# Own-key blocks of a squared-relu attention: half of the second step's weights read back turned from DRAM instead of computed

## The chip, the cores and the metric

The kernel runs on one core of a Trainium2 chip. The time is the device time of one execution in microseconds. Before the change it was 1749.55 us, the median of 3 runs (1749.34 to 1753.78). All profile rows come from one profiled execution. PE is TensorE's matmuls, PEld its weight loads, DVE VectorE, ACT ScalarE, POOL GpSimd, SP SyncE; SPq is SyncE's DMA queue.

## The reference

Eight batches of 2496 rows. Attention takes z both as queries and as keys, so its scores are symmetric, and then each row goes past a gate to one of eight experts:

```python
scores = (1.0 / S) * np.matmul(z, z.transpose(0, 2, 1))   # z: 8 x 2496 x 64
attn = np.maximum(scores, 0.0) ** 2
x = (u * np.matmul(attn, v)).reshape(B * S, D)            # u, v: 8 x 2496 x 256

do_compute = x @ w_skip > 0                               # rows that go to an expert
e_idx = np.argmax(x[do_compute] @ w_gate, axis=1)         # 8 experts, 256 -> 1024 -> 256
y = gate_w * (np.maximum(xc @ w1[e], 0.0) @ w2[e])
out[do_compute] = x[do_compute] + y                       # the other rows: out = x
```

All inputs are fp32. The kernel keeps nearly fp32 accuracy on TensorE by splitting each operand into a high and a low part and adding three products: high by high, high by low, low by high.

## The kernel before

**Attention, the first 1200 us or so.** A batch's queries are cut into 5 chunks (0 to 4), four of 512 and the last of 448. The keys come in 10 groups of 256, called p; so there are 8 x 5 x 10 = 400 steps, each one chunk of queries against one group of keys. The key groups p = 2c and p = 2c+1 are the chunk's own keys: the block in which keys and queries are the same rows of z. ORDER gives the order of the ten steps of a chunk; for chunks 1 to 4 the own group 2c is the first step (k = 0) and 2c+1 the last (k = 9).

A step makes its weights and then uses them:

- `scores`: six matmuls 64x512 (L277) give the scores of 256 keys by 512 queries in PSUM, `ps`. Each product runs on two 64-row halves of TensorE, which hold different keys.
- ScalarE takes the relu into the tile `r` (L325, 128x1024 in fp32) and squares it (L326).
- The high part `ah` is a cast of `r` (L335, on ScalarE or VectorE as `on_act` says); the low part `al` is the difference (L339, VectorE).
- `attend` (L366): twelve matmuls for each half d of the 256 columns of v, with `ah` or `al` streaming into the accumulators `acc`.

Weights are made two steps ahead of their use (`LA = 2`), by `stage`. There are 5 buffers for `r`, 3 each for `ah` and `al`, 2 in PSUM for `ps`.

**Symmetry between chunks.** The weights of keys in block j by queries in block c are the transpose of those of keys in c by queries in j. So the chunk that comes first computes its block, VectorE turns it in 32x32 pieces (`keep`, L294, tile `rt`), four puts of 256 KB write it to a DRAM tile `kept` (L728, by `put_some`, which is called once at the end of a step and issues at most four puts, of entries that are at least one step old, two in chunks 1 to 4), and the chunk that comes later reads it back ready (`recall`, L310, or L312 and L313 for the last chunk of 448), with no scores, relu or square. The recall is issued by `ahead(s + LA + 3)`, five steps before the step that uses it and three before that step's weights are staged. The own blocks are not in this scheme: both own-key steps of a chunk compute all their scores. In batch 0, the first chunk's blocks are not kept.

**What sets the order.** All engines' programs are recorded in the order of the code; each engine runs its own in that order. All transfers of `r`, `rt`, the loads of u and v (L168, L97), the rows stored after a chunk (L416 in four puts of 128 KB with 256-byte pieces, L412) are issued by SyncE, whose queue also keeps that order. A chunk's rows are stored at step 4 of the next chunk.

**The end of a chunk.** At k = 9 the accumulators are copied out (L394, ScalarE, into `xrow`, and L396, VectorE) and turned (L403); the next chunk's first two steps are staged around that.

**The MoE part, to the end.** Rows are gathered by expert through index lists; h (L638) and y (L657) are three matmuls per product, again high and low; relu (L643, ScalarE) and its low part (L644, VectorE).

Of the kernel before, what the change touches and what calls it, by code (L numbers as in the profile page):

```python
# [8 lines left out]
F32 = mybir.dt.float32  # L9
# [3 lines left out]
AF = mybir.ActivationFunctionType  # L13
# [4 lines left out]
P = 128  # L18
QC = 512
# [4 lines left out]
NFIX = 3  # L24
HT = 64
NARM = 4 * (NSTAT - NFIX)
NWARM = 52

# [14 lines left out]
def f32(ap):  # L45
    return ap.bitcast(F32)
# [3 lines left out]
def attn_moe(ctx, tc, zT, uT, v, wg, w1, w2, cst, pad, out):  # L50
# [4 lines left out]
    nc = tc.nc  # L55
    B, _, SZ = zT.shape
    S = uT.shape[3]
    D = 2 * P
# [5 lines left out]
    isc = 1.0 / S  # L64

    chunks = []
# [5 lines left out]
    dram = ctx.enter_context(tc.tile_pool(name="dram", bufs=1, space=bass.MemoryType.DRAM))  # L72
    vp = ctx.enter_context(tc.tile_pool(name="vp", bufs=1))
# [14 lines left out]
    zt, vt = {}, {}  # L88
# [85 lines left out]
    ones = cpool.tile([P, P], BF16, name="ones")  # L174
    nc.gpsimd.memset(ones, 1.0)
    psw = ps_s.tile([P, 2, QC], F32, name="psw", tag="s")
    for _ in range(NWARM):
        nc.tensor.matmul(psw[:32, 0, :70], ones[:, :32], ones[:, :70], start=True, stop=True)

    f0 = load_z(0, 0, nc.vector)  # L180
    f1 = load_v(0, 0, nc.vector)
# [59 lines left out]
        return (j, c) in pairs(b) or (c, j) in pairs(b) or p in EXTRA[c]  # L241

    kept = {x: dram.tile([QC, QC], F32, name="kept%d%d" % x) for x in PAIRS}
    HALF = (slice(0, 64), slice(64, 128))

    zq = {}

# [13 lines left out]
    def queries(ci, k, h, n):  # L261

        if ci in zq:
            return zq[ci][k][h, :n]
        return zt[ci // NQ, ci % NQ][k][h].rearrange("p (b a i) -> p a b i", b=4, a=4)

    def scores(ci, p):

# [11 lines left out]
    def r_tile():  # L280
        return ap.tile([P, 2, QC], F32, name="r", tag="r", bufs=5)
# [3 lines left out]
    def keep(ci, p, r):  # L285
# [12 lines left out]
        if p % 2:  # L298

            dst = kept[c, j].rearrange("(m i) k -> i m k", i=32)  # L300
            for a in range(4):
                puts.append((step[0], dst[:, :, a * P : a * P + P], t[32 * a : 32 * a + 32]))

    def recall(ci, p):

        r = r_tile()
        src = kept[p // 2, ci % NQ].rearrange("(k p) q -> p k q", k=4)
        src = src[:, p % 2 * 2 : p % 2 * 2 + 2, :]
        if chunks[ci][2] == QC:
            nc.sync.dma_start(r, src)  # L310
        else:
            nc.sync.dma_start(r[:, :, :352], src[:, :, :352])  # L312
            nc.sync.dma_start(r[:, :, 352:448], src[:, :, 384:480])  # L313
        return r
# [3 lines left out]
    def weights(ci, p, r=None, at_end=False):  # L318

        b, q0, n = chunks[ci]  # L320
        old, new = r, (ci % NQ, p // 2) in pairs(b)
        if not old:
            ps = scores(ci, p)
            r = r_tile()
            nc.scalar.activation(r[:, :, :n], ps[:, :, :n], AF.Relu, scale=isc)  # L325
            nc.scalar.activation(r[:, :, :n], r[:, :, :n], AF.Square)  # L326
        views, got = [], []

        def high():
            ah = ap.tile([P, 2, QC], F32R, name="ah", tag="ah")  # L330
            al = ap.tile([P, 2, QC], F32R, name="al", tag="al")
            got.extend((ah, al))
            views.append([x[:, :, :n] for x in (r, ah, al)])
            for r_, h_, _ in views:
                (nc.scalar.copy if on_act(ci, p) else nc.vector.tensor_copy)(h_, r_)  # L335

        def low():
            for r_, h_, l_ in views:
                nc.vector.tensor_sub(l_, r_, f32(h_))  # L339
            if new:  # L340
                if at_end:
                    put_off.append(lambda: keep(ci, p, r))
                else:
                    keep(ci, p, r)

        return got, high, low
# [383 lines left out]
    def ahead(s):  # L730
        if s < len(steps):
            ci, p = steps[s]
            if (p // 2, ci % NQ) in pairs(ci // NQ):
                old[s] = recall(ci, p)
                known.add(s)


    def later(s, k, load, *args):
        def start():
# [57 lines left out]
    for s, (ci, p) in enumerate(steps):  # L797
        b, q0, n = chunks[ci]
        k = s % NP
        step[0] = s  # L800
        ahead(s + LA + 3)
        if k == 0:
            accs[ci] = [[ps_acc.tile([P, QC], F32, name="acc", tag="acc") for _ in range(2)] for _ in range(2)]
        acc = accs[ci]
        if k < NP - 1:
            high, low = stage(s + LA)
            if k < NP - 2 or s + LA in known:
                high()
                low()
                high = low = lambda: None  # L810
            while k == NP - 3 and put_off:
                put_off.pop()()
            attend(b, n, p, 0, acc[0], *aa[s], k == 0, False)
            for t in () if k in (0, NP - 2) else (s - 1, s) if k == 1 else (s,):
                attend(b, n, steps[t][1], 1, acc[1], *aa.pop(t), t % NP == 0, False)
            rest = high, low
        else:


            part, mul, rows0, rows1, store = finish(ci)  # L820
            attend(b, n, p, 0, acc[0], *aa[s], False, True)

            high, low = rest
            if s + 1 < len(steps) and not on_act(*steps[s + 1]):
                high()
                low()
                high = low = lambda: None
            part(0, 1, acc[0])
            part(0, 0, acc[0])
            high()  # L830
            low()
            high, low = stage(s + LA)
            attend(b, n, steps[s - 1][1], 1, acc[1], *aa.pop(s - 1), False, False)
            if s + LA in known:

                high()
                low()
                high = low = lambda: None
            attend(b, n, p, 1, acc[1], *aa.pop(s), False, True)
            part(1, 1, acc[1])  # L840
            high()
            part(1, 0, acc[1])
            low()
            mul()
            accs.pop(ci)

            new.append(ci)
            if ci < NC - 1:
                after = [(rows0, 2), (rows1, 3), (store, 4), (store, 8)]
                if ci % 2 == 0:  # L850
                    gates, logits, route, counts, gate, place, put_in = routing(new)
                    after = [(gates, 2), (logits, 2), (rows0, 2), (rows1, 3), (route, 4), (counts, 4),
                             (store, 4), (gate, 5), (place, 6), (store, 8)]
                    for t in range(0, 4 * len(new), 2):
                        f = lambda put_in=put_in, t=t: put_in(t, t + 2)
                        if s + 6 + t < len(steps):
                            after.append((f, 6 + t))
                        else:
                            left.append(f)
                    new = []  # L860
                for f, k in after:
                    todo.setdefault(s + k, []).append(f)
            else:
                gates, logits, route, counts, gate, place, put_in = routing(new, False)
        for f in todo.pop(s, []):
            f()
        put_some()
# [200 lines left out]
```

## Time and profile before

| | |
|---|---|
| profiled execution | 1750.08 us, span 1748.3 us |
| runs | 1749.55 us median (1749.34 to 1753.78) |
| mean granted TensorE clock | 0.998 |
| TensorE busy | 1729.9 us, 99% of the span |
| VectorE, ScalarE, GpSimd busy | 1187.8, 1131.5, 519.8 us |
| scores, relu and square | 248 times each on ScalarE |
| full recalls | 90 of 512 KB, median 6.5 us from issue to landing |
| puts of turned blocks | 304 of 256 KB, median 4.8 us |

In a row of a timeline the first number is the start in us from the span's start, the second the length, then engine, line, operation, tiles (output <- input), shape and how many instructions the row stands for; in brackets the idle time before it and what ended that. For a DMA the row is its issue, not its transfer. A row of a window gives its bounds and length, busy time of PE, PEld, DVE, ACT and POOL with instruction counts, the granted clock, the mean busy share of the DMA engines, and GB/s. A row of the waits gives the total idle time, the number of waits and the longest.

### The profile page before, as it was taken

The page shows a single profiled execution, that of the slowest core. Times are in us where ns is not written, and L with a number is a line of the kernel's source. Part 1 is how long each engine was busy: PE and PEld are TensorE (multiplying, and loading weights), DVE is VectorE, ACT ScalarE, POOL GpSimd, SP SyncE. Part 2 cuts the span into 40 slices and gives each one's busy share as a digit, 9 for nine tenths or more (in the row PEclk, how much of TensorE's full clock was granted, in tenths as well). Part 3 has the DMA queues.
Part 4 walks back from the last instruction along what each step waited for, and adds up shares of the span by engine and source line. Part 5 has one row for each costly group of instructions (what it writes and reads, how often), then busy time and mean ns, then how long its engine had stood idle before and what let it go on. Part 6 is the DMA issues. An engine that isn't in the chain of part 4 may idle for free. (4 is left out here: it accounts for less than half of the span.)

```text
span 1748.3 us, 39163 instructions
## 1 busy us (share of the span) xinstructions
PE 1729.9 (99%) x15476; PEld 1531.0 (88%) x15476; DVE 1187.8 (68%) x1928; ACT 1131.5 (65%) x1409; POOL 519.8 (30%) x516
## 2 busy tenths in 40 slices
PE   9999999999999999999999999999999999999998
PEld 7888788988888898888889888888999999999997
DVE  7877877887887788788778877877753334344332
ACT  8877877887687778768787876887533323333321
POOL 1103202212311221231222032122256456635731
PEclk9999999999999999999999999999999999999999
DMA  5566779577867858885785888586653333323310
GB/s 194 151 180 173 187 209 275 136 221 233 216 167 202 251 162 231 230 234 148 206 250 163 212 240 228 138 223 190 202 128 81 86 88 106 91 59 97 85 42 26
DMA packets 373514, 294.71 MB, mean 169 GB/s; under 512 B 136432, under 2 KB 311409, under 8 KB 372560
## 3 DMA queue, kind: packets, MB, share of 16 engines
q1 hardware_dynamic: 359136, 267.85, 55.4%
q0 software_dynamic: 13632, 22.99, 4.6%
q8 instruction: 137, 2.24, 0.5%
q14 instruction: 177, 1.45, 0.3%
q10 hardware_dynamic: 432, 0.18, 0.0%
HBM read 177.92 MB, written 133.79 MB: 178 GB/s over the span
## 5 line engine op out<-in xcount | busy, mean ns | idle before, releaser
L366 PE MATMUL acc<-ah,vh 64*128 64x512 f32 (+1 forms) x3120 | 641.5, 384 | 2.7 <-DVE ah L335 2.0
L366 PE MATMUL acc<-ah,vl 64*128 64x512 f32 (+1 forms) x3120 | 626.4, 382 | 0.0
L339 DVE TENSOR_TENSOR al<-r,ah 128x1024 fp32r<-128x1024 f32 (+1 forms) x400 | 479.2, 1204 | 169.6 <-ACT ah L335 163.1
L366 PE MATMUL acc<-al,vh 64*128 64x512 f32 (+1 forms) x3120 | 498.2, 384 | 1.9 <-DVE al L339 1.2
L537 POOL DMA_INDIRECT lst<-pair,dest x160 | 200.0, 1250 | 769.1 <-DVE dest L535 685.1
L335 ACT CAST ah<-r 128x1024 fp32r<-128x1024 f32 (+1 forms) x356 | 362.8, 1030 | 80.9 <-PE acc L366 43.4
L366 PEld LDWEIGHTS acc<-ah,vh 64*128 64x128 f32 x3120 | 326.8, 184 | 56.0 <-ACT ah L335 4.3
L366 PEld LDWEIGHTS acc<-ah,vl 64*128 64x128 f32 x3120 | 327.1, 184 | 44.5 <-DVE vl L122 0.3
L366 PEld LDWEIGHTS acc<-al,vh 64*128 64x128 f32 x3120 | 309.5, 184 | 56.3 <-DVE al L339 11.7
L325 ACT ACTIVATE r<-ps 128x1024 f32<-128x1024 f32 (+1 forms) x248 | 252.7, 1019 | 147.2 <-PE ps L277 129.1
L643 ACT ACTIVATE hh<-psh 128x512 fp32r<-128x512 f32 (+2 forms) x172 | 97.0, 571 | 282.6 <-PE psh L638 261.2
L326 ACT ACTIVATE r<-r 128x1024 f32<-128x1024 f32 (+1 forms) x248 | 261.4, 1054 | 7.9
L657 PE MATMUL y<-w2t,hh 128*128 128x256 f32 (+1 forms) x1328 | 235.0, 280 | 0.0
L644 DVE SCALAR_TENSOR_TENSOR hl<-psh,hh 128x512 fp32r<-128x512 f32 (+2 forms) x172 | 110.2, 655 | 146.7 <-ACT hh L643 130.2
L294 DVE STREAM_TRANSPOSE rt<-r 128x512 f32<-128x512 f32 x304 | 197.3, 687 | 9.4 <-DMA kept<-rt 8.5
L657 PEld LDWEIGHTS y<-w2t,hh 128*128 128x128 f32 (+1 forms) x1328 | 200.5, 185 | 1.3
L638 PE MATMUL psh<-xt,w1h 128*128 128x256 f32 (+3 forms) x896 | 184.6, 303 | 2.9 <-DVE hl L644 2.9
L657 PE MATMUL y<-w2t,hl 128*128 128x256 f32 (+1 forms) x664 | 184.2, 277 | 0.0
L638 PEld LDWEIGHTS psh<-xt,w1h 128*128 128x128 f32 x896 | 141.7, 189 | 8.5 <-DVE hl L644 4.4
L638 PE MATMUL psh<-xt,w1l 128*128 128x256 f32 (+3 forms) x448 | 135.0, 301 | 0.0
L689 POOL DMA_INDIRECT out<-o,idt x77 | 76.5, 994 | 164.2 <-DVE o L686 131.9
L657 PEld LDWEIGHTS y<-w2t,hl 128*128 128x128 f32 (+1 forms) x664 | 122.6, 185 | 0.0
(188 smaller groups left out, 1706.7 us busy)
## 6 DMA issues: line engine op xcount, KB each, us to landing
kept<-rt SPq DMA_DIRECT2D x304, 256.0 KB, 4.8
r<-kept SPq DMA_DIRECT2D x90, 512.0 KB, 6.5
r<-kept SPq DMA_DIRECT2D x62, 352.0 KB, 5.6
raw<-in_v SPq DMA_DIRECT2D x80, 256.0 KB, 5.5
ut<-in_uT SPq DMA_DIRECT2D x32, 512.0 KB, 5.8
xr<-xrow SPq DMA_DIRECT2D x128, 128.0 KB, 3.1
out<-xr SPq DMA_DIRECT2D x32, 512.0 KB, 6.8
raw<-in_w SPq DMA_DIRECT2D x64, 256.0 KB, 3.3
```

Source lines behind the costliest of these rows:

```text
L294: nc.vector.transpose(t[:, :, 32 * k : 32 * k + 32].rearrange("p (k a) i -> p a k i", k=4), r[:, x, :].rearrange("p (a k i) -> p a k i", a ...
L325: nc.scalar.activation(r[:, :, :n], ps[:, :, :n], AF.Relu, scale=isc)
L326: nc.scalar.activation(r[:, :, :n], r[:, :, :n], AF.Square)
L335: (nc.scalar.copy if on_act(ci, p) else nc.vector.tensor_copy)(h_, r_)
L339: nc.vector.tensor_sub(l_, r_, f32(h_))
L366: nc.tensor.matmul(acc[t][:, :n], w[h, x, dd], a[h, x, :n], start=(first and t not in halves[:m]), stop=(last and t not in halves[m + 1 :]),)
L537: put = nc.gpsimd.indirect_dma_start(out=lst, out_offset=bass.IndirectOffsetOnAxis(ap=dest[:, t : t + 1], axis=0), in_=pair[:, t, :], in_o ...
L638: nc.tensor.matmul(ps[:, j * W : (j + 1) * W], wt[:, a, o : o + P], x[:, d, :W], start=(m == 0), stop=(m == 5),)
L643: nc.scalar.activation(hh[:, : G * W], ps[:, : G * W], AF.Relu)
L644: nc.vector.scalar_tensor_tensor(hl[:, : G * W], ps[:, : G * W], 0.0, f32(hh[:, : G * W]), op0=ALU.max, op1=ALU.subtract)
L657: nc.tensor.matmul(ys[t], h[:, tt], w2t[f][:, k, :], start=(f == 0 and m == 0 and t % share == 0), stop=(f == NF - 1 and m == 2), skip_gro ...
L689: put = nc.gpsimd.indirect_dma_start(out=out, out_offset=bass.IndirectOffsetOnAxis(ap=ids[:m, t, 0:1], axis=0), in_=ot, in_offset=None, bo ...
```

## The change

The own block is symmetric in itself. With its 512 rows split in two, the first own-key step (keys 0 to 255, p = 2c) holds among others the weights of keys 0 to 255 by queries 256 to 511; turned, they are those of keys 256 to 511 by queries 0 to 255, which is half of the second own-key step (p = 2c+1). For chunks 1, 2 and 3 of every batch (24 places) the change

- turns that half at the end of the first own-key step (`keep_half`, two VectorE transposes of 128 partitions by 256, into a tile `rd` that takes a buffer of the loads' tag "raw") and puts it to a DRAM tile of 256x256 by four puts of 64 KB, through the same list of puts;
- reads it into the lower half of the second own-key step's `r` (`recall_half`, two DMAs of 128 KB whose pieces in SBUF are 256 bytes), issued by `half_ahead(s + LA + 1)`, three steps before the use, right behind the full recall that `ahead` issues in the same step;
- computes scores for the other half of the queries alone (`scores_half`, six matmuls of 256 columns in place of 512), with relu and square of half the size. The cast and everything behind it are as before, on the whole tile.

The warming matmuls at the start go from 52 of 70 columns to 53 of 69.

```diff
+    kept_d = {c: dram.tile([QC // 2, QC // 2], F32, name="kept%d" % c) for c in range(1, S // QC)}
+    def own(ci, p):
+        b, c = ci // NQ, ci % NQ
+        return p % 2 if c in kept_d and p // 2 == c else None
+    def upper(x):
+        return x.rearrange("p x (a j) -> p x a j", a=4)[:, :, :, 64:]
+    def scores_half(ci, p):
+        b, _, _ = chunks[ci]
+        ps = ps_s.tile([P, 2, QC], F32, name="ps", tag="s")
+        zh, zl = zt[b, p // 2]
+        for m, (k, q) in enumerate(((zh, 0), (zh, 1), (zl, 0))):
+            for x, h in enumerate(HALF):
+                o = (2 * p + x) % 4 * P
+                nc.tensor.matmul(
+                    ps[:, x, : QC // 2].rearrange("p (a j) -> p a j", a=4), k[h, o : o + P],
+                    queries(ci, q, h, QC).rearrange("p (a j) -> p a j", a=4)[:, :, 64:],
+                    start=(m == 0), stop=(m == 2),
+                )
+        return ps
+    def keep_half(ci, r):
+        c = ci % NQ
+        t = vp.tile([P, 2, D], F32, name="rd", tag="raw", bufs=4).rearrange("p x (k i) -> p (x k) i", i=64)
+        for x in range(2):
+            nc.vector.transpose(
+                t[:, :, 32 * x : 32 * x + 32].rearrange("p (k a) i -> p a k i", k=2),
+                r[:, x, :].rearrange("p (a k i) -> p a k i", a=4, k=4)[:, :, 2:],
+            )
+        dst = kept_d[c].rearrange("(m i) k -> i m k", i=32)
+        for a in range(4):
+            puts.append((step[0], dst[:, :, 64 * a : 64 * a + 64], t[32 * a : 32 * a + 32]))
+    def recall_half(ci):
+        r = r_tile()
+        for x in range(2):
+            nc.sync.dma_start(
+                r[:, x].rearrange("p (a j) -> p a j", a=4)[:, :, :64],
+                kept_d[ci % NQ][x * P : x * P + P].rearrange("p (a j) -> p a j", a=4),
+            )
+        return r
...
-        if not old:
+        if own(ci, p) == 1:
+            ps = scores_half(ci, p)
+            part = ps[:, :, : QC // 2].rearrange("p x (a j) -> p x a j", a=4)
+            nc.scalar.activation(upper(r), part, AF.Relu, scale=isc)
+            nc.scalar.activation(upper(r), upper(r), AF.Square)
+        elif not old:
...
+            if own(ci, p) == 0:
+                todo.setdefault(step[0] + 1, []).append(lambda: keep_half(ci, r))
...
+    def half_ahead(s):
+        if s < len(steps) and own(*steps[s]) == 1:
+            old[s] = recall_half(steps[s][0])
...
         ahead(s + LA + 3)
+        half_ahead(s + LA + 1)
```

SyncE's queue in chunk 1 of batch 4, before: the rows of the chunk ahead (xr, L416), four puts of a turned block, then a full recall, the load of u and further recalls. (The numbers behind `kept_` count DRAM tiles, and are one higher after the change.)

```order
L416 DMA xr<-xrow 32x16x64 x4
L728 DMA kept_195<-rt 32x16x128 x4
L310 DMA r<-kept_191 128x2x512
L168 DMA ut<-in_uT 128x2x512
L310 DMA r<-kept_191 128x2x512
L412 DMA out<-xr 16x8192
```

The same place after the change:

```order
L472 DMA xr<-xrow 32x16x64 x4
L784 DMA kept_201<-rd 32x8x64 x4
L784 DMA kept_196<-rt 32x16x128 x4
L359 DMA r<-kept_192 128x2x512
L347 DMA r<-kept_201 128x4x64 x2
L168 DMA ut<-in_uT 128x2x512
L359 DMA r<-kept_192 128x2x512
L468 DMA out<-xr 16x8192
```

The four puts of the half (`kept_201<-rd`) stand ahead of the four of the whole block; its two reads stand behind the full recall and ahead of u.

SyncE's queue in chunk 2 of the same batch, before:

```order
L97 DMA raw<-in_v 128x512
L416 DMA xr<-xrow 32x16x64 x4
L728 DMA kept_197<-rt 32x16x128 x4
L310 DMA r<-kept_192 128x2x512
L168 DMA ut<-in_uT 128x2x512
L310 DMA r<-kept_195 128x2x512
L412 DMA out<-xr 16x8192
```

and after:

```order
L784 DMA kept_202<-rd 32x8x64 x4
L97 DMA raw<-in_v 128x512
L472 DMA xr<-xrow 32x16x64 x4
L784 DMA kept_198<-rt 32x16x128 x4
L359 DMA r<-kept_193 128x2x512
L347 DMA r<-kept_202 128x4x64 x2
L168 DMA ut<-in_uT 128x2x512
L359 DMA r<-kept_196 128x2x512
L468 DMA out<-xr 16x8192
```

Here the puts of the half go out ahead of a load of v and of the rows; the two reads again stand right behind the full recall.

More of the change, by code (lines that the diff above doesn't have):

```diff
@@ L26 @@
 NARM = 4 * (NSTAT - NFIX)
-NWARM = 52
+NWARM = 53
 PAIRS = ((0, 1), (0, 2), (0, 3), (0, 4), (1, 2), (1, 3), (1, 4), (2, 3), (2, 4), (3, 4))
@@ L177, in attn_moe @@
     for _ in range(NWARM):
-        nc.tensor.matmul(psw[:32, 0, :70], ones[:, :32], ones[:, :70], start=True, stop=True)
+        nc.tensor.matmul(psw[:32, 0, :69], ones[:, :32], ones[:, :69], start=True, stop=True)
     f0 = load_z(0, 0, nc.vector)
```

## The prediction

> **What bounds the kernel now.** I read the page's busy times first, then the stages by window, and then the timeline of each engine around the own-key steps of the three middle chunks. The page says that TensorE has almost no idle time (first row; the second, from the chain of waits, prices a matmul of 256 columns):
>
> ```profile
> PE 1729.9 (99%) x15476; PEld 1531.0 (88%) x15476; DVE 1187.8 (68%) x1928; ACT 1131.5 (65%) x1409; POOL 519.8 (30%) x516
> 1626.95 5.46 PE y L657 x48
> ```
>
> So every column that TensorE no longer streams is time, and every moment for which it waits is time too. The change does both: it takes columns away and gives TensorE a transfer to wait for. The two must be priced apart.
>
> **The gain per place.** The six score matmuls of an own-key step stand as three rows of two ahead of the next attend row (chunk 2 of batch 4, TensorE's timeline):
>
> ```profile
> 724.40 0.39 PE L277 MATMUL ps<-zqh,zh 64*128 64x512 f32 x2
> ...
> 725.08 0.39 PE L366 MATMUL acc<-ah,vh 64*128 64x512 f32 x2
> ```
>
> From 724.40 to 725.08 are 0.68 us, 0.227 a pair; the two matmuls of a pair use different 64-row halves and run side by side. At 256 columns no pair is in this trace; the nearest row is the chain's 5.46 us for 48 matmuls of 128x256, 0.114 each. If a pair goes down to that, a place saves 3 x (0.227 - 0.114) = 0.34 us. There are 24 places (8 batches, chunks 1 to 3): **8.2 us**. The lower bound is no gain, if the weight loads, which are as many as before, don't fit behind a matmul of half the length. What a load takes is seen where one could not hide, behind a stall:
>
> ```profile
> 1098.37 0.47 PE L366 MATMUL acc<-ah,vh 64*128 64x448 f32 x2 [1.18 <-DVE ah L335]
> 1098.68 0.36 PE L366 MATMUL acc<-ah,vl 64*128 64x448 f32 x2
> ```
>
> The first pair is 0.11 us longer than the second: two loads of 64x128 side by side cost 0.11, just less than 0.114. I take the full 0.34, and keep 0 for the range. The Trainium skill ("TensorE: Matmul & The Clock Gate", Part 3) says that a weight load overlaps with matmuls in flight only when its row group differs. By that rule a pair here would take load and matmul one after the other, 0.11 + 0.23 = 0.34; the trace disagrees, with 0.227. At 256 columns that rule would leave 0.11 + 0.114 = 0.22 a pair and no gain.
>
> **What moves to other engines.** VectorE gets two more transposes of half a tile at the end of the first own-key step; the whole one is 0.69 us, so the two are between 0.7 and 1.4 (half price, or no gain from the smaller size). ScalarE's relu and square go from 1.03 and 1.06 to the size of the 0.57 row: about 0.95 us less a place.
>
> ```profile
> L294 DVE STREAM_TRANSPOSE rt<-r 128x512 f32<-128x512 f32 x304 | 197.3, 687 | 9.4 <-DMA kept<-rt 8.5
> L643 ACT ACTIVATE hh<-psh 128x512 fp32r<-128x512 f32 (+2 forms) x172 | 97.0, 571 | 282.6 <-PE psh L638 261.2
> 681.32 1.23 DVE L339 TENSOR_TENSOR al<-r,ah 128x1024 fp32r<-128x1024 f32 x1 [1.38 <-ACT ah L335]
> ```
>
> VectorE idles 1.38 us in the third row, ahead of the low part at the start of chunk 1, and that cover takes the transposes; uncovered they would delay the next low part by at most 1.4 us. I take 0. The saving on ScalarE counts only if the cast behind it may start, and this cast now waits for the recalled half. That is the term that decides.
>
> **When the half comes back.** SyncE's queue issues in program order, and the new transfers stand there: four puts of 64 KB in 256-byte pieces, and two reads of 128 KB of which each lands in 256-byte pieces, placed right behind the chunk's full recall (L310). Nearest prices:
>
> ```profile
> r<-kept SPq DMA_DIRECT2D x90, 512.0 KB, 6.5
> 714.00:717.00 3.00, 3.00 (x30) 2.49 (x28) 1.39 (x2) 2.97 (x4) 0.54 (x1) 1.00 0.80 166
> 719.00:723.00 4.00, 4.00 (x38) 3.33 (x36) 2.04 (x3) 3.94 (x5) 0.00 (x0) 1.00 0.81 190
> 726.00:728.00 2.00, 2.00 (x20) 1.68 (x18) 0.58 (x1) 1.94 (x3) 1.77 (x4) 1.00 0.98 342
> ```
>
> (The last three are windows; the last two numbers are the DMA engines' busy share and GB/s.) 714 to 717 is the store of rows in 256-byte pieces: 166 GB/s at 0.80, so 208 at full share. 719 to 723 is puts in 512-byte pieces, 235 at full share; 726 to 728 reads in 2-KB pieces, 342 at 0.98. So 256 KB of 256-byte pieces occupy the engines for 1.26 us (0.75 at the read rate, the lower bound). The Trainium skill ("DMA: Bandwidth & Descriptors", Specifications) puts the line rate at 512 bytes and more, and so speaks against this change; the trace agrees in direction, with 208 against 342 GB/s at full share. Packets leave in the order of issue: the half lands after the full recall in front of it.
>
> *Chunk 2.* SyncE, ScalarE, VectorE and the weight loads, batch 4:
>
> ```profile
> 718.08 3.40 SPq L728 DMA_DIRECT2D kept<-rt  x4
> 721.58 1.40 SPq L310 DMA_DIRECT2D r<-kept  x1
> ...
> 727.44 1.05 ACT L335 CAST ah<-r 128x1024 fp32r<-128x1024 f32 x1
> ...
> 729.84 1.03 ACT L325 ACTIVATE r<-ps 128x1024 f32<-128x1024 f32 x1 [0.83 <-DVE al L339]
> ...
> 733.43 0.19 PEld L366 LDWEIGHTS acc<-ah,vh 64*128 64x128 f32 x2 [0.45 <-ACT ah L335]
> ACT r L325 <- DVE al L339: 6.3, 7, 1.4
> ```
>
> This chain has no slack: the cast at 727.44, its low part on VectorE, the next chunk's first relu, which waits for that part (0.83), and after that relu's square and cast the weight loads that wait for them (0.45). The last row, from the list of waits, has that relu wait seven times: once in each of batches 1 to 7. A cast that starts later than 727.44 moves TensorE by as much. The full recall was issued at 721.58; with the 6.5 us of the median it lands at 728.1, with the 5.98 of this one at 727.6. The half lands 0.75 to 1.8 us behind it: 728.3 to 729.9, so 0.9 to 2.4 us late. I take 1.3 (recall at 727.6, as timed here, and the half 1.26 behind it), seven times: **+9.1**.
>
> *Chunk 1:*
>
> ```profile
> 684.38 2.21 SPq L416 DMA_DIRECT2D xr<-xrow  x4
> 687.20 3.59 SPq L728 DMA_DIRECT2D kept<-rt  x4
> 690.89 1.39 SPq L310 DMA_DIRECT2D r<-kept  x1
> ...
> 696.96 1.05 ACT L335 CAST ah<-r 128x1024 fp32r<-128x1024 f32 x1
> ...
> 698.04 1.22 DVE L339 TENSOR_TENSOR al<-r,ah 128x1024 fp32r<-128x1024 f32 x1 [1.10 <-ACT ah L335]
> ...
> 699.17 0.61 PE L366 MATMUL acc<-ah,vh 64*128 64x512 f32 x2
> ```
>
> The step's weights are first used at 699.17 and their low part about 0.9 later, so the cast may start by 697.7, 0.75 later than it does. But here the four puts of the half stand between the row stores (L416) and the puts of L728. Four row stores, each of twice the bytes in pieces of the same size, keep SyncE for 2.21 us; the four puts then take between half of that, 1.1, and all of it. The recall of 690.89 goes to 692.0 at the earliest and 693.1 at the latest and with 6.0 us lands at 698.0 to 699.1; the half, 0.75 to 1.26 behind it, at 698.7 to 700.4. Against 697.7 that is 1.0 to 2.7; I take 1.5, nearer the lower end because the puts are half the size, seven times: **+10.5**.
>
> *Chunk 3:*
>
> ```profile
> 750.10 0.58 SPq L312 DMA_DIRECT2D r<-kept  x1
> 750.73 0.73 SPq L313 DMA_DIRECT2D r<-kept  x1
> ...
> 758.17 1.06 ACT L335 CAST ah<-r 128x1024 fp32r<-128x1024 f32 x1
> ```
>
> Here the half is issued at about 751.5 and with 6.5 us lands by 758.0, in time for 758.17. The eight places there, and the two of chunks 1 and 2 in batch 0, which recalls nothing from its first chunk, keep their gain: 10 x 0.34 = **-3.4**. At the 14 late places the gain of 0.34 is TensorE's own work and is swallowed by the wait, since the landing sets the time.
>
> **The clock.** The one long stall of before, of 1.18 us and then more, was followed by a stretch at a lower granted clock (the number before the last two):
>
> ```profile
> 1100.00:1105.00 5.00, 5.00 (x36) 4.52 (x34) 2.57 (x4) 3.12 (x6) 0.00 (x0) 0.67 0.01 3
> ```
>
> 5 us at 0.67 cost about 1.7 us. How often a stall of 1.3 to 1.5 us does this can't be told from one case; of 14 I take one: **+1.7**.
>
> **Sum.** -3.4 + 9.1 + 10.5 + 1.7 = +17.9 on the profiled execution's 1750.08 us, of which the span is 1748.3; the median of the runs, 1749.55, is 0.5 under it. I take 2 us off, because a TensorE that stalls in chunk 1 lets ScalarE and VectorE get ahead for the steps behind it, and forecast **1766 us**. This case's own range: the lower bounds, 7 x 0.9 + 7 x 1.0 - 3.4 = +9.9 less those 2, give 1758; the upper, 7 x 2.4 + 7 x 2.7 - 3.4 + 3 x 1.7 = +37, 1787.
>
> **Rivals.**
> *The half lands in time* (faster). For it: the DMA engines are at 0.80 in the stretches before, so the half could slip into gaps and land with the recall, or ahead of it. Against: the share of 0.98 from 726 to 728, just when chunk 2's half would be moved. It decides if the half lands before 727.4 in chunk 2 and 697.7 in chunk 1. Then all 24 places gain: 1750.1 - 8.2 = 1741.9, and to 1739 if the seven waits of 0.45 go too.
> *A little late.* With 0.2 to 0.5 us late at 14 places, +2.8 to +7, less 3.4: about 1751.
> *The weight loads don't hide at half length.* A pair then stays at 0.22: 1750 with the half in time, 3.4 more than the forecast with it late. What speaks against it is the 0.11 of the loads above. The rule of the Trainium skill that stands there would bring it about.
> *Late, and the clock drops at most places.* 12 more windows of 1.7 us on the forecast: about 1786.
> *The change doesn't do what it says* would be, here, scores still computed in full width; the instruction list has them at half, so I give it nothing.
>
> **How the numbers follow.** 0.3% of 1749.55, 5.2 us, is about what can be told from no change: faster is below 1744.3, slower above 1754.8. Chances: the forecast 0.52, the lower clock at most places 0.06, a little late 0.13 (of which 0.02 over 1754.8), loads that don't hide 0.04 (0.02 in time, the same; 0.02 late, slower), in time 0.25. So slower 0.62, same 0.13, faster 0.25. The range of 8 in 10 takes in the case on the other side: 1740 to 1786; the forecast's own is 1758 to 1787.
>
> **What would show it.** Right: in the profile after, the cast of the second own-key step's weights waits for the read of the half in chunks 1 and 2, by 1 us and more, in batches 1 to 7, and TensorE's idle time grows by some 20 us there; chunk 3 shows no such wait. The score rows of that step should be 0.11 us apart; at 0.2 the gain is gone. Wrong: no wait at those casts, with TensorE's busy time 8 us down, which would mean that the landing is not in the order of issue or that a 256-byte read is cheaper than its nearest row; or waits on VectorE's transposes, which I cost at nothing.

## The result and the profile after

The changed kernel took 1795.65 us (median of 4 runs, 1791.14 to 1800.45), the one before 1750.84 us on the same chip (1749.34 to 1753.78, 4 runs): the ratio is 1.0254, with a 95% interval of 1.0221 to 1.0288. It is **45 us slower**, where 16 were forecast; the direction was right, the time lies above the range. The profiled execution is one of 1791.14 us, with a span of 1789.3 and a clock of 0.994 (before 0.998).

First the busy times of the changed kernel, then, from the lists of the costliest groups, the attend matmuls and the casts, before (L366, L335) and after (L422, L389).

```profile
PE 1740.6 (97%) x15477; PEld 1546.6 (86%) x15477; DVE 1204.8 (67%) x1976; ACT 1111.3 (62%) x1409; POOL 516.1 (29%) x516
L366 PE MATMUL acc<-ah,vh 64*128 64x512 f32 (+1 forms) x3120 | 641.5, 384 | 2.7 <-DVE ah L335 2.0
L335 ACT CAST ah<-r 128x1024 fp32r<-128x1024 f32 (+1 forms) x356 | 362.8, 1030 | 80.9 <-PE acc L366 43.4 <-DMA r<-kept 29.6 <-ACT vh L121 1.7
L422 PE MATMUL acc<-ah,vh 64*128 64x512 f32 (+1 forms) x3120 | 669.1, 387 | 31.2 <-ACT ah L389 29.1
L389 ACT CAST ah<-r 128x1024 fp32r<-128x1024 f32 (+1 forms) x356 | 363.0, 1029 | 142.1 <-DMA r<-kept 106.3
```

The casts now wait 106.3 us for reads of turned blocks, where it was 29.6, and TensorE waits 29.1 us for casts ahead of these attend matmuls, where it was idle for 2.7 in all. Its busy time has risen, by 10.7 us, although it streams fewer columns: it worked more slowly somewhere.

The gain itself is there. The half-width scores of chunk 1, batch 4, on TensorE's timeline:

```profile
715.67 0.28 PE L285 MATMUL ps<-zqh,zh 64*128 64x256 f32 x2
715.78 0.28 PE L285 MATMUL ps<-zql,zh 64*128 64x256 f32 x2
715.90 0.28 PE L285 MATMUL ps<-zqh,zl 64*128 64x256 f32 x2
716.02 0.40 PE L422 MATMUL acc<-ah,vh 64*128 64x512 f32 x2
```

Six matmuls take 0.35 us in place of 0.68; the pairs are 0.11 to 0.12 apart.

Then the same place further on: SyncE's queue, ScalarE, TensorE.

```profile
706.33 2.21 SPq L472 DMA_DIRECT2D xr<-xrow  x4
708.58 3.00 SPq L784 DMA_DIRECT2D kept<-rd  x4
711.68 3.55 SPq L784 DMA_DIRECT2D kept<-rt  x4
715.33 1.44 SPq L359 DMA_DIRECT2D r<-kept  x1
716.94 1.72 SPq L347 DMA_DIRECT2D r<-kept  x2
...
717.38 0.63 ACT L375 ACTIVATE r<-r 128x512 f32<-128x512 f32 x1
722.54 1.04 ACT L389 CAST ah<-r 128x1024 fp32r<-128x1024 f32 x1 [4.52 <-DMA r<-kept]
...
723.64 0.50 PE L422 MATMUL acc<-ah,vh 64*128 64x512 f32 x2 [2.90 <-ACT ah L389]
```

The four puts of the half (`kept<-rd`) hold SyncE for 3.00 us. The full recall is issued 9.0 us behind the first row store, where it had been 6.5; the half is issued behind that, the cast waits 4.52 us for it, and TensorE then stands still for 2.90 us.

To see where the 41 us of span went, the two traces were paired matmul by matmul (15,424 of them, in the same order in both programs, the warming ones left out): the start in the trace after less the start in the trace before. How much that difference grows from just ahead of the own-key scores to a few steps behind them:

```
us gained (-) or lost (+)   batch 0    1     2     3     4     5     6     7    sum of 1 to 7
chunk 1                      +0.59  +4.63 +6.29 +4.67 +3.18 +5.07 +2.85 +4.19    +30.9
chunk 2                      -0.30  +1.07 +2.64 +1.25 +1.07 +1.97 +1.15 +0.76     +9.9
chunk 3                      -0.28  -0.27 +1.91 +0.64 -0.30 +0.13 -0.30 -0.20     +1.6
```

At each of the 24 places the scores give 0.33 us first (0.23 to 0.25 at three of them). Chunk 1 then loses it many times over; chunk 2 loses about what was forecast, chunk 3 little. All else in the program adds up to -1.

The slower work of TensorE is in the windows behind the stalls of chunk 1 (batches 2, 3, 4 and 5; the number before the last two is the granted clock, which stayed at 1.00 in batch 4):

```profile
396.00:400.00 4.00, 3.57 (x16) 2.80 (x18) 2.49 (x4) 2.96 (x5) 0.82 (x1) 0.50 0.27 75
561.00:565.00 4.00, 3.44 (x18) 2.70 (x20) 2.57 (x4) 3.24 (x5) 0.00 (x0) 0.61 0.87 277
723.00:727.00 4.00, 3.29 (x26) 2.44 (x28) 3.18 (x5) 3.90 (x5) 0.62 (x1) 1.00 0.91 264
882.00:886.00 4.00, 4.00 (x22) 2.82 (x24) 3.09 (x4) 3.41 (x4) 0.00 (x0) 0.60 0.86 292
```

Summed over windows of 4 us up to 1320, the granted clock costs 10.3 us in the trace after ((1 - clock) x 4 for each window) and 1.7 before. All of it is behind the stalls of chunk 1, in five of the seven batches, in stretches of about 3.4 us at half the clock. The table above shows their price: chunk 1 lost 3.18 and 2.85 us in batches 4 and 6, which had none, 4.19 to 5.07 in the four batches with one, and 6.29 in batch 2, which had two.

### The profile page after: what moved, and what is told of

The parts are those of the page before. It is cut to its first block, busy times and chain, and to the rows that moved or that the text cites. A ratio compares the mean times of both kernels' runs of the same rounds, so it can differ in the third digit from the quotient of the medians.

```text
span 1789.3 us, 39410 instructions
## 1 busy us (share of the span) xinstructions
PE 1740.6 (97%) x15477; PEld 1546.6 (86%) x15477; DVE 1204.8 (67%) x1976; ACT 1111.3 (62%) x1409; POOL 516.1 (29%) x516
## 4 chain that ended last, share of the span: by engine, by line
PE 74%; DMA 10%; ACT 7%; DVE 4%; issue 3%; SPq 1%; POOL 0%; DVEq 0%; ACTq 0%; POOLq 0%
PE acc L422 43%; PE y L713 11%; PE psh L694 11%; PE ps L302 7%; DMA r<-kept 6%; DVE al L393 3%; ACT ah L389 2%; ACT r L379 2%; DMA out<-o,idt 2%; ACT r L380 2%; PE psm L494 1%; PE pst L660 1%; DVE rt L319 1%; DMA raw<-in_v 1%; SPq L347 0%
## 5 line engine op out<-in xcount | busy, mean ns | idle before, releaser
L422 PE MATMUL acc<-ah,vh 64*128 64x512 f32 (+1 forms) x3120 | 669.1, 387 | 31.2 <-ACT ah L389 29.1
L422 PE MATMUL acc<-ah,vl 64*128 64x512 f32 (+1 forms) x3120 | 654.5, 384 | 0.0
L422 PE MATMUL acc<-al,vh 64*128 64x512 f32 (+1 forms) x3120 | 524.5, 387 | 2.4 <-DVE al L393 1.1
L389 ACT CAST ah<-r 128x1024 fp32r<-128x1024 f32 (+1 forms) x356 | 363.0, 1029 | 142.1 <-DMA r<-kept 106.3
L422 PEld LDWEIGHTS acc<-ah,vh 64*128 64x128 f32 x3120 | 358.3, 186 | 86.3 <-ACT ah L389 40.1
L422 PEld LDWEIGHTS acc<-ah,vl 64*128 64x128 f32 x3120 | 358.3, 186 | 40.3 <-DVE vl L122 0.3
L422 PEld LDWEIGHTS acc<-al,vh 64*128 64x128 f32 x3120 | 331.1, 185 | 57.6 <-DVE al L393 17.3
L379 ACT ACTIVATE r<-ps 128x1024 f32<-128x1024 f32 (+1 forms) x224 | 228.0, 1018 | 136.9 <-PE ps L302 127.5
L380 ACT ACTIVATE r<-r 128x1024 f32<-128x1024 f32 (+1 forms) x224 | 235.9, 1053 | 7.1
```

Of the source, the lines that this page charges most:

```text
L422: nc.tensor.matmul(acc[t][:, :n], w[h, x, dd], a[h, x, :n], start=(first and t not in halves[:m]), stop=(last and t not in halves[m + 1 :]),)
```

## The experiments

Chips differ: the kernel before took 1747 to 1760 us on the four chips that these runs were given, so each number below is a difference from the kernel before in runs on the same chip. Where that chip has no trace of the kernel before, traces are paired with the first one.

**One chunk at a time.** The edit (here for chunk 1):

```diff
-    kept_d = {c: dram.tile(...) for c in range(1, S // QC)}
+    kept_d = {c: dram.tile(...) for c in (1,)}
```

> The half recalled in chunk 1 alone (8 places of 24). Theory L (the landing of the half in chunk 1 sets the time, and the long stalls bring the lower clock with them): in the changed kernel, matmul by matmul against the one before, the seven stretches around chunk 1 of batches 1 to 7 give +31 us together; so +28 to +33 here, about 1781 us. Rival: the stall in chunk 1 is fed by the transfers of chunks 2 and 3, as the DMA engines are busy throughout; then less than +20.

> The half recalled in chunk 2 alone. Theory L: the seven stretches around chunk 2 of batches 1 to 7 gave +10 us in the changed kernel; here +8 to +11, about 1760 us, with the cast waiting about 1.8 us for the half. Rival: chunk 2 is late only because of what chunk 1 left behind; then -2.6 (8 places of 0.33), about 1748.

> The half recalled in chunk 3 alone, where it lands in time. Theory L: 8 x 0.33 us less, 1748 us, and no wait of the cast for the half. Rival: the transfers themselves cost something wherever they are put (other recalls land later): 1751 us or more.

Measured, against 1758.47 us: chunk 1 alone +31.0 us (ratio 1.0186, 1.0166 to 1.0205), chunk 2 alone +8.9 (1.0062, 1.0039 to 1.0084), chunk 3 alone +1.1 (1.0009, 1.0000 to 1.0019). Together 41 us, near the 45 of all three at once on the first chip: chunks 1 and 2 are each late by themselves. Chunk 3 was expected at -2.7 and missed that, though the paired trace has -0.30 us at six of its eight places and -0.01 and -0.16 at the two others. Where the rest went stays open: two executions of this one kernel differ by more (1756.25 to 1762.08).

**Work in the stall.** In chunk 1 of batches 1 to 7 the half-width scores are computed eight times over:

```diff
-        for m, (k, q) in enumerate(((zh, 0), (zh, 1), (zl, 0))):
+        again = 8 if b and ci % NQ == 1 else 1
+        for m, (k, q) in again * list(enumerate(((zh, 0), (zh, 1), (zl, 0)))):
```

> All 24 places, with the half-width scores of chunk 1 in batches 1 to 7 computed eight times over (seven needless repeats of 0.34 us, 2.4 us of TensorE work a place, ahead of the stall). Theory L with the clock: the landing sets the time, so the work disappears in the stall, and TensorE isn't idle long enough for the lower clock; the time falls by the 7 us or so that the five slow stretches cost, to 1788 us. Rival C (the lower clock doesn't come from the stall): no change, 1796. Rival P (TensorE's own work sets the time there): +17, 1812.

Measured +35.5 us (1.0215, 1.0191 to 1.0239), against +41.0 for the three chunks on that chip. So 17 us of added matmuls cost nothing: what sets the time there is the landing. The windows at batches 2 and 3:

```profile
396.00:400.00 4.00, 3.90 (x31) 2.66 (x30) 3.22 (x6) 3.89 (x6) 0.91 (x1) 1.00 0.81 221
556.00:560.00 4.00, 3.60 (x22) 2.58 (x24) 3.13 (x4) 3.81 (x5) 0.00 (x0) 0.77 0.41 103
```

Where the work filled the stall the clock stayed at 1.00; only batch 3, with 1.94 us of idle left, fell. So the lower clock comes with the stall. The time that this gave back, 5.5 us, is near the 7 expected, but the two numbers come from separate kernels with intervals of 2 to 3 us each. By the traces the lower clock fell from 10.3 to 1.7 us up to the MoE part, while chunk 1 lost 27.2 us in place of 30.9: the cast came 0.6 us later in the median, 16.6 us behind the first row store in place of 16.0, and so part of the gain was lost again.

**Order at SyncE.** Two edits, each alone and both together: the half read ahead of the full recall; and, in chunk 1, the puts of the half issued a step earlier, ahead of the row stores.

```diff
-        ahead(s + LA + 3)
-        half_ahead(s + LA + 1)
+        half_ahead(s + LA + 1)
+        ahead(s + LA + 3)
```

```diff
-        for _ in range(4):
+        for _ in range(8 if step[0] % (NP * NQ) == NP + 2 else 4):
             if puts and puts[0][0] < step[0] - (step[0] // NP % NQ > 0):
```

> All 24 places; one edit: the two reads of the half are issued ahead of the full recall of the same step, not behind it. Theory L (landing in the order of issue): in chunk 1 the half lands some 1.6 us earlier, so the stall goes from 2.9 to about 1.3 us and mostly loses its slow clock; in chunk 2 it lands before it is needed. 7 x 1.3 and 7 x 0.4 for what follows a stall, less the gain at 17 places (0.33 each): about +7, between +3 and +12. Rival: the stall in chunk 1 is SyncE's, which comes late to the recalls because of the four puts ahead; then the order of the two changes little (SyncE needs 1.4 us for the full recall): +30 or more.

> All 24 places; one edit: in chunk 1 the four puts of the half are issued one step earlier, ahead of the stored rows, where SyncE waited 3.6 us for nothing but the rows. Theory L: the full recall is back where it was (6.5 us behind the first row store, not 9.0), and the half comes 2.5 us earlier: the stall in chunk 1 goes from 2.9 to 0.4 us, with no slow clock; chunk 2 keeps its +1.1 a batch. 7 x 0.5 + 7 x 1.1 - 3.3: about +8, between +4 and +13. Rival: the puts aren't the cause (the DMA engines have so much to move in any case); then +30 or more.

> Both edits together. Theory L: the half lands in time in chunks 1 and 2; all 24 places gain 0.33 us: -8, between -9 and -4, since the full recall behind the half comes 1 to 2 us later than before the change, and some of that may be missed by the step that it serves. Rival: the transfers cost as much wherever they stand; +5 or more.

> The kernel before, for a profile on the same chip: no difference. It shows what the start of the MoE part costs on this chip (in the runs of one chunk alone TensorE waited some 12 us there for nothing that the profile shows), and whether the long stall of chunk 3 in batch 6 comes again.

Measured, against 1760.08 us: half first +21.3 (1.0118, 1.0101 to 1.0135), puts early +35.8 (1.0202, 1.0182 to 1.0222), both +9.8 (1.0052, 1.0034 to 1.0069). All three were slower than expected, puts early by far; puts early and both lie in the bands of their rivals. Paired with the trace of the kernel before from that chip, the stretches of batches 1 to 7 give

```
                   chunk 1   chunk 2   chunk 3
half first          +10.8      -2.1      -1.6
puts early          +22.4     +10.3      -0.8
both                 +2.6      -2.6      +0.1
```

So chunk 2 is cured by the order of the two reads. The places sum to +7.1 for half first, which is what was expected of the whole, and to +0.1 for both, where -8 was expected. What these two runs lose beyond that, 14 and 10 us, lies elsewhere. With the half first, the paired trace stands at +13.6 us where the MoE part begins; 5.3 of that are seven short delays in chunk 4. With both edits it stands at +2.5 us there and at +9.1 at the end. In the MoE part TensorE waits for nothing that the profile shows on this chip, but in the kernel before as well (8.6 us in all, 9.1 with both edits):

```profile
1258.40 0.50 PE L638 MATMUL psh<-xt,w1h 128*128 128x256 f32 x2 [0.83 <-issue]
1259.92 0.37 PE L638 MATMUL psh<-xt,w1l 128*128 128x256 f32 x1 [0.31 <-issue]
1260.63 0.27 PE L638 MATMUL psh<-xt,w1h 128*128 128x256 f32 x1 [0.23 <-issue]
```

What differs there is the lower clock: five stretches of 3.4 us with both edits, two in the kernel before, which makes 5.1 of the 6.6 us. Whether that is chance, two profiled executions can't tell.

**What the puts hold up.** Chunk 1 alone, without the puts (after batch 0), and with the puts but without the read:

```diff
-            puts.append((step[0], dst[:, :, 64 * a : 64 * a + 64], t[32 * a : 32 * a + 32]))
+            if ci < NQ:
+                puts.append((step[0], dst[:, :, 64 * a : 64 * a + 64], t[32 * a : 32 * a + 32]))
```

```diff
-        if own(ci, p) == 1:
+        if False:
             ps = scores_half(ci, p)
...
-        half_ahead(s + LA + 1)
```

> Chunk 1 alone, with the puts of the half left out after batch 0 (so the reads bring batch 0's block, and the output is another); reads, half-width scores and the turns stay. Theory Q (what stands ahead in the DMA queue sets the landing): the full recall is back at its place, 2.5 us earlier, and the half behind it lands some 0.7 us late: +3 to +8, where chunk 1 whole gave +31. Rival: the half is late for its own reads and the full recall ahead of it; then +25 or more.

> Chunk 1 alone, with the turns and the puts of the half, but it isn't read: full scores, as before. Theory Q: the puts alone delay the full recall by 2.5 us, which its step has to spare; 0 to +4. Rival: the puts cost the time by themselves, by whatever they hold up: +15 or more.

Measured, against 1747.17 us: without puts +7.6 (1.0041, 1.0023 to 1.0059), without the read -0.7 (0.9993, 0.9982 to 1.0004). Both came out as expected. The puts are worth 23 of chunk 1's 31 us, but only through the read that waits behind them: alone they cost nothing. SyncE's queue without them:

```profile
688.17 2.21 SPq L473 DMA_DIRECT2D xr<-xrow  x4
690.98 3.69 SPq L785 DMA_DIRECT2D kept<-rt  x4
694.77 1.39 SPq L360 DMA_DIRECT2D r<-kept  x1
```

The full recall is back at 6.6 us behind the row stores. The 7.6 us that stay are the half's own: it still lands behind the full recall, 0.8 to 1.0 us in the four batches whose landings the trace tells. Nor does the read wait for the puts to land: in the changed kernel, in batch 4, SyncE issues it 0.17 us after the full recall (716.77 to 716.94), and the puts, which land 3.0 us behind their issue in the median, had been issued by 711.58.

**SyncE's time, or the DMA engines'?** Three more of chunk 1 alone: the same bytes in larger pieces, the puts a step early (the edit above), and both.

```diff
-        dst = kept_d[c].rearrange("(m i) k -> i m k", i=32)
+        dst = kept_d[c].rearrange("(q r) k -> q (r k)", r=2)
         for a in range(4):
-            puts.append((step[0], dst[:, :, 64 * a : 64 * a + 64], t[32 * a : 32 * a + 32]))
+            h = slice(32 * a, 32 * a + 32)
+            puts.append((step[0], dst[h], t[h].rearrange("p m i -> p (m i)")))
...
-                r[:, x].rearrange("p (a j) -> p a j", a=4)[:, :, :64],
-                kept_d[ci % NQ][x * P : x * P + P].rearrange("p (a j) -> p a j", a=4),
+                r[:, x, : QC // 2], kept_d[ci % NQ][x * P : x * P + P],
...
```

The half-width scores then go to the upper 256 columns of `r` in one piece (two lines, not shown).

> Chunk 1 alone, with the same bytes in larger pieces: puts in pieces of 2 KB and reads into 1 KB of SBUF, in place of 256 bytes (the turned values then land at wrong places, and the output is another). If the 256-byte pieces are what makes the half late, puts fall from about 2.0 to 0.8 us and reads from 1.4 to 0.8: the stall goes from 2.9 to about 1.1 us, without the slow clock: +6 to +14. Rival (the bytes count, in whatever pieces): +25 or more.

> Chunk 1 alone, puts of 256-byte pieces issued a step earlier, ahead of the row stores. Theory T (two limits in a row: SyncE's issue and the DMA engines' backlog): the issue of the full recall goes back to 6.4 us behind the first row store, but its data still stands behind 256 KB of small pieces; +20 to +28, against +31 where only chunk 1 is changed. Rival I (SyncE's issue alone): 0 to +8.

> Both: puts a step earlier and all pieces larger (values land at wrong places, the output is another). Theory T: with both limits lifted the cast starts some 4.3 us behind the half's scores (3.7 would be in time), as it did without any puts (4.5) or a little better: +1 to +8. Rival B (the bytes in the queue count, whatever their pieces and their place): +15 or more.

```
chunk 1 alone        pieces of 256 bytes             larger pieces
puts where they are  +31.0 (1.0186)                  +21.3 (1.0106; 1.0086 to 1.0127)
puts a step early    +16.1 (1.0088; 1.0067 to 1.0110)  +7.3 (1.0052; 1.0030 to 1.0075)
```

The whole time of the two kernels with larger pieces can't be held against the others. Their values are wrong, so rows go to other experts, and their MoE part has 80 matmuls fewer. The busy times of early puts, with 256-byte and with larger pieces, on the same chip:

```profile
PE 1742.4 (98%) x15477; PEld 1542.8 (87%) x15477; DVE 1196.1 (67%) x1944; ACT 1123.0 (63%) x1409; POOL 519.1 (29%) x516
PE 1734.8 (98%) x15397; PEld 1544.8 (88%) x15397; DVE 1191.2 (68%) x1937; ACT 1120.8 (64%) x1403; POOL 516.3 (29%) x515
```

From the first matmul of h to the last of y the MoE part takes 486.2 us there in place of 497.2, and on the other chip 477.7 where the kernel without the puts takes 482.0. The paired traces of the attention part don't have this fault. In chunk 1 of batches 1 to 7 they give

```
                             lost    of that lower clock   rest
256 bytes, in their place    +28.9          8.5            20.4
larger, in their place       +25.1         10.2            14.9
256 bytes, a step early      +15.4          3.4            12.0
larger, a step early         +12.0          1.7            10.3
no puts                       +7.3          0               7.3
```

Larger pieces were expected at +6 to +14 or, by the rival, over 25: the traces are with the rival. Early puts were expected at +20 to +28 or 0 to +8, and lie between. Both together do not come to what is left without any puts: the cast starts 5.1 us behind the half's scores in the median, where theory T had 4.3 and the kernel without puts has 4.3 (6.7 with the puts in their place). So of the 13 us, without the clock, that the puts cost, issuing them early takes off 8.4, larger pieces 5.5, or 1.7 where the puts are early; each figure rests on one execution. With all three chunks changed, early puts took less off: 30.9 in chunk 1 became 22.4.

SyncE's time and the DMA engines' are not two separate causes, though. In the changed kernel SyncE takes 1.8 to 2.2 us for the four puts of chunk 2, and 2.2 to 3.0 (median 2.5) for those of chunk 1, right behind the row stores; issued early, right behind the four puts of a whole block, it takes 3.5 to 3.8. Larger pieces change that little: a median of 2.3 behind the row stores, 3.6 early. Batch 4 of the kernel with larger pieces:

```profile
695.87 2.19 SPq L472 DMA_DIRECT2D xr<-xrow  x4
698.11 3.02 SPq L784 DMA_DIRECT2D kept<-rd  x4
701.23 3.52 SPq L784 DMA_DIRECT2D kept<-rt  x4
704.85 1.35 SPq L359 DMA_DIRECT2D r<-kept  x1
```

The issue takes longer the more was queued just ahead of it. What in the queue holds SyncE (its length, or its writes) none of the runs tells.

And with early puts the batches go two ways. SyncE's queue in batches 1 and 2, first of the kernel before, then with early puts in chunk 1 alone:

```profile
212.55 3.46 SPq L728 DMA_DIRECT2D kept<-rt  x4
218.37 0.90 SPq L416 DMA_DIRECT2D xr<-xrow  x2
...
366.54 3.42 SPq L728 DMA_DIRECT2D kept<-rt  x4
373.59 0.83 SPq L416 DMA_DIRECT2D xr<-xrow  x2
```

```profile
213.18 3.47 SPq L784 DMA_DIRECT2D kept<-rt  x4
216.74 3.79 SPq L784 DMA_DIRECT2D kept<-rd  x4
220.63 3.08 SPq L472 DMA_DIRECT2D xr<-xrow  x4
...
371.34 3.42 SPq L784 DMA_DIRECT2D kept<-rt  x4
374.87 3.73 SPq L784 DMA_DIRECT2D kept<-rd  x4
378.69 2.32 SPq L472 DMA_DIRECT2D xr<-xrow  x4
```

SyncE waits for the rows 2.36 us in batch 1 (216.01 to 218.37) and 3.63 in batch 2. In the odd batches the puts, 3.79 us, don't fit and push the row stores and all behind them; in the even ones, with 3.73 us, they all but fit. The paired traces have the same pattern: +4.23, +2.06, +4.13 and +2.59 in batches 1, 3, 5 and 7, and +0.59, +0.38 and +1.42 in 2, 4 and 6. With larger pieces too, the odd batches lose 1.7 to 4.1 us there and the even ones 0.1 to 0.9. The expectation had been drawn from batch 4, with 3.7 us of room, and taken for all.

**A version without chunk 1:**

```diff
-    kept_d = {c: dram.tile(...) for c in range(1, S // QC)}
+    kept_d = {c: dram.tile(...) for c in (2, 3)}
...
+        first = ci % NQ == 2
+        if first:
+            half_ahead(s + LA + 1)
         ahead(s + LA + 3)
-        half_ahead(s + LA + 1)
+        if not first:
+            half_ahead(s + LA + 1)
```

> The half in chunks 2 and 3 alone; in chunk 2 read ahead of the full recall, in chunk 3 behind it. By the stretches of the earlier runs chunk 2 then gives -2.9 and chunk 3 -2.3: 5 us faster than the kernel before, between -6 and -2. Rival: the full recall that now comes later in chunk 2 costs a stall elsewhere: 0 or more.

Measured -0.2 us (1.0002, 0.9988 to 1.0015): no difference, and a miss. The paired trace has -1.8 us in chunk 2 of batches 1 to 7 and +2.1 in chunk 3, where in batch 5 a cast waits for the read and TensorE stalls for 1.57 us. No version was found that beats the kernel before.

## Why the prediction was wrong

*The gain per place* was right: 0.33 us measured, 0.34 forecast. By the rule of the Trainium skill ("TensorE: Matmul & The Clock Gate", Part 3), that weight loads overlap only with matmuls of another row group, a pair would have stayed at 0.22, by the prediction's estimate; the trace has 0.11 to 0.12.

*Transposes on VectorE at nothing, less work on ScalarE* was right, as far as shown: no stall is put down to them, and the turns and puts alone came to -0.7 us.

*Chunk 2* was right: +9.1 forecast, +9.9 measured, and the remedy, the order of the two reads, works as the mechanism says. The cast was forecast 1.3 us late (its own terms, 727.6 and 1.26 against 727.44, give 1.4). Over batches 1 to 7 it starts 16.75 us behind the first row store in the median, where it was 15.45 before; batch by batch it is 0.8 to 2.5 us later, 1.35 in the mean. That the mean fits so well is in part luck.

*Chunk 1* is the step that failed: +10.5 forecast, and +1.7 for one stretch of lower clock in the whole program; +30.9 measured, 10.2 of it lower clock. Its mechanism was right (the puts push the full recall, the half lands behind it, TensorE waits). Two terms were too small: what the four puts cost at SyncE, and the clock. Medians over batches 1 to 7, from the first row store:

```
                       before   after   without puts   half first   puts early   both
full recall issued       6.41    8.56       6.38         11.24         6.48       9.24
half issued                -    10.37       7.88          8.59         7.84       6.56
cast of the step        12.40   16.02      13.60         14.23        13.95      11.57
half's scores start      9.14    9.13       9.14          9.13         7.70       7.77
```

First, the puts. They were costed at 1.1 to 2.2 us of SyncE from the row stores, taking the number of bytes and pieces as the measure, and the lower end was preferred because the puts are half the size. They took 2.5 us in the median and 3.00 in batch 4, from which the forecast was drawn: more than the row stores themselves, with twice the bytes. The full recall is issued 2.15 us later in the median and 2.49 in batch 4, as a pause of SyncE took up some of it (0.6 us in batch 4): that is the upper end of what the forecast allowed, and beyond it in batch 4. The other terms held: the recall lands 6.0 to 6.3 us behind its issue and the half 1.0 to 1.1 behind the recall, in the three batches whose landings the trace tells. In chunk 2 of the same batch four such puts took less,

```profile
733.37 1.89 SPq L784 DMA_DIRECT2D kept<-rd  x4
```

so it is not their own bytes that set it. The cast comes 3.6 us later than before; 0.75 of that was free by the forecast, so it is 2.9 late, not 1.5, and a little above the upper bound of 2.7. Seven times 2.9 are 20.3 us, and 20.7 are what chunk 1 lost without the clock.

The 0.75 was generous: without the puts the cast comes 0.7 to 2.1 us later than before and costs 0.6 to 1.8 a batch. Nor is TensorE's idle time the whole of a stall: in batch 4, where the clock didn't fall, the idle is 2.90 us and the pairing shows 3.56 lost behind the scores. The ends of matmuls in the profile are modelled, which may cover the rest; that isn't shown.

Second, the clock. One stretch was forecast and six came, in five batches: 10.2 us in place of 1.7. The row from which it was priced, behind a stall of 1.18 us, is no fixed trait of the kernel before either: its second trace has neither that stall nor that stretch. The rival "late, and the clock drops at most places" had this, at 1786 us, with a chance of 0.06. It was priced on the forecast's too short stalls.

*The 2 us taken off* for engines that get ahead had no row behind them and aren't seen. *Chunk 3 and batch 0* were forecast at -3.4 and came to +1.6. Six of the ten places gained 0.20 to 0.30; four lost time. In chunk 1 of batch 0 (+0.59) no full recall stands ahead, but the eight puts do, and the cast waited 1.48 us for the half. In chunk 3 of batch 3 (+0.64) the cast waited 2.19 us for a read. In batch 2 (+1.91) the stall comes later, at a recall of chunk 4. Batch 5 (+0.13) wasn't followed up.

With at most 2.4 us a place in chunk 2 and 2.7 in chunk 1, and three lower-clock stretches, the range ended at 1787. The choice of 1.5, near the lower end, was wrong, and the upper bound too tight: the nearest row, four row stores, had been issued after SyncE had waited 3.7 us, and the puts come right behind those stores.

## What to carry to other kernels

When a transfer is put in front of others in one queue, cost the whole queue behind it: the same four puts took SyncE 1.9 or 3.8 us, by what had been issued just ahead of them, and the last transfer in line pays it. Look at every batch for the room in the queue, not at one; here it alternated between some 2.3 and 3.7 us. And where TensorE is 99% busy, a stall of 2 us or more is to be priced with a stretch at the lower clock: in the changed kernel it followed five of seven such stalls, and a stretch cost 1.7 us.

## What the runs showed that was not expected

The lower clock follows stalls of very different length, and not every time. In the trace after, TensorE's idle of 2.35, 2.84, 2.91, 3.18 and 4.01 us was followed by it, 2.51 and 2.90 us weren't; with the stall filled, 1.94 us was and 1.46 wasn't; in other runs 1.69 us was (puts early) and 1.97 wasn't (half first). The Trainium skill ("TensorE: Matmul & The Clock Gate", HAM oscillation) advises against idle gaps of more than about 3.4 us; here gaps from 1.69 us on were followed by the lower clock at times, so the measurement goes below the rule. No run with two stalls of chosen length tells whether it is the place in a fixed window that decides.

The size of pieces matters less than expected. The Trainium skill ("DMA: Bandwidth & Descriptors", Specifications) puts the line rate at 512 bytes and more. Going from 256 bytes to 1 and 2 KB took 28.9 us in chunk 1 to 25.1, or 20.4 to 14.9 without the lower clock: the rule's direction, but an eighth to a quarter of the loss.

In the MoE part TensorE loses 6 to 10 us to waits that the profile shows only as "issue" on three of the five chips, in the kernel before as well (8.6 us), and nothing on the two others. Their cause is not known.
